# Output product 4 by a second Strassen level, its quarters in a bank of their own, and ReLUs and x's sums at other steps

## The chip, the cores and the metric

The kernel runs on one core of a Trainium2 chip. The time is the device time of one execution in microseconds (us), and the number compared is the median over several executions. Four engines matter here: TensorE (PE, with PEld for its weight loads), VectorE (DVE), ScalarE (ACT) and GpSimd (POOL). SyncE (SP) starts the DMA transfers that read, ScalarE's queue those that write the output.

## The reference, cut to what matters

```python
kv  = einsum('bhsd,bhse->bhde', k, v)          # q, k, v: (8, 8, 576, 64)
out = einsum('bhsd,bhde->bhse', q, kv)         # no softmax
out = out / sqrt(mean(out*out, -1) + 1e-6) * g_norm
x = out.transpose(0, 2, 1, 3).reshape(4608, 512)
h = x @ w_in                                   # 512 -> 2048
g = maximum(0.01 * h, h)
return g @ w_out                               # 2048 -> 512
```

Everything is float32. The two large products, x by w_in and g by w_out, take most of the time.

## The kernel before

The 4608 tokens are worked on in nine blocks of 512. Block 0 goes the plain way (`first_block`). In blocks 1 to 8 (the loop variable i) the 2048 columns of h are taken in four chunks c of 512, so that a chunk has an h product (512 x 512 by 512 x 512) and an output product of the same size, which is added to the block's four output quarters. I number the output products n = 4(i - 1) + c. They wait in `o_queue`: product n begins at the third step (`LAG` = 2 steps) of the chunk after its h, and ends with the second step of the chunk after that.

Both products are done with Strassen's scheme in Winograd's form: seven products of half size (256 x 256 x 256) in the order `ORDER = (1, 2, 6, 5, 7, 3, 4)` instead of eight. One PSUM bank takes 1, 6, 7 and 4 in turn, a second 2, 5 and 3; since each new product is accumulated on the last in the bank, output quarter 11 is 1 + 2, quarter 12 is 1 + 6 + 5 + 3 and so on, and after each step what stands in the bank is copied out or added to its quarter (`strassen`, `done`). The sums that the scheme needs as operands are made ahead: those of g by GpSimd in `sums_of` (tiles `gs`, 128 x 512), those of w_out once, then kept in DRAM and loaded for each chunk by `sums` in `sides_w2` (tiles `t12` and `t34`, 512 KB each, from SP's queue).

In blocks 2 to 8 the h product has a second level (`product_h_two`): each of the seven steps is again seven products of 128 x 128 blocks, four in one bank (j = 1, 6, 7, 4) and three in another (j = 2, 5, 3), with weights from a ring of five places that SP refills (448 KB each). After each step ScalarE copies (k = 1, 6, 5 and 4, line 951) or VectorE adds (k = 2, 7 and 3, helper `add`, line 636) the seven quarters into `qa` and `qc`. When the seven steps are over, seven sums on VectorE make the four quarters of g, `relu` (line 832, ScalarE) is applied to each, and GpSimd makes the four sums of `sums_of`.

The bank of three has a free fourth column. Output product 2 of the products n = 4 to 29 is done in it by a second level (class `Second`): one quarter product of 128 columns is put behind each h step of a later chunk. So in the order of an output product of that kind the place of product 2 is empty: `(1, 5, 6, None, 7, 3, 4)`. Its inner operands are made by GpSimd: `inner_g` (128 x 128 adds at steps 4 and 6) and, in block 2, `inner_w2`.

A chunk has seven steps t, and the block 28 slots, 7c + t. In a step the program gives out, in this order: one h step; at t = 6 the first of the g sums as well; pieces of the attention of a later block at the slots of `FINE_SLOTS` and `LATE_SLOTS`; at slots 20 to 22 x's inner sums for the next block on VectorE (`sides_x`), at 24 and 25 further inner sums on GpSimd; loads; `inner_g`; then one step of the output product. At the chunk's end the rest of the h product follows: the remaining g sums, the four ReLUs and `sums_of`. `pin` keeps an instruction in program order on its engine; what is not pinned the scheduler places when its operands are ready. All matmuls go through the helper of line 118 and most element-wise sums through line 636, so groups are told apart by the names of their tiles.

| name | what it is |
|---|---|
| h_ha, h_hb, h_hc, h_hd | PSUM banks of h steps (even: ha and hc of four, hb and hd of three quarters) |
| o_a, o_c | PSUM banks of the output products |
| pairs | one tile that holds `qc`, `t12`, `t34` and `gi` (inner sums of g) |
| w_all, stage | w1's ring, `qa` and x's sums |
| g, gs | the quarters of g, and GpSimd's sums of them |

The output quarters of a block are accumulated in SBUF (tag "o", six buffers). ScalarE copies the fresh ones at c = 0 and stores each one (256 KB) after the last product of chunk 3 that goes into it.

Of the kernel before, what the change touches and what calls it, by code (L numbers as in the profile page):

```python
# [23 lines left out]
def kernel(  # L24
# [74 lines left out]
    NW = U * NE * P  # L99
    w1_all = consts.tile([P, 2 * NC * NW], F32, name="w1_all")  # L100
    stage = consts.tile([P, 3 * NW], F32, name="stage")
    pairs = consts.tile([P, 4 * NW], F32, name="pairs")
    g_all = [consts.tile([P, 4 * U * N2], F32, name=f"g_{i}") for i in range(2)]

    def view(t, lo, *shape):
# [79 lines left out]
    zeros = view(g_all[0], 0, NT)  # L185
    nc.vector.memset(zeros[:, :64], 0.0)
    nc.vector.memset(zeros[:, 64:], 0.0)
    ident = consts.tile([P, P], F32, name="ident")

    def make_ident():  # L190
        pin(nc.gpsimd.memset(ident, 1.0))
# [448 lines left out]
    def sides_w1(c):  # L640
# [9 lines left out]
        def more():  # L650
# [5 lines left out]

    w2_dram = [[dram.tile([P, 2, U, N2], F32, name=f"w2_{c}_{i}") for i in range(2)]
               for c in range(NC)]
    t12, t34 = pair(2, 2, U, N2), pair(3, 2, U, N2)
    writes = []  # L660

    def sides_w2(n):

        c = n % NC
        b11, b12 = w2_sb[0][c][:, :, :N2], w2_sb[0][c][:, :, N2:]
        b21, b22 = w2_sb[1][c][:, :, :N2], w2_sb[1][c][:, :, N2:]

        def sums(i):  # L670
            t = (t12, t34)[i]
            if n >= NC:
                pin(nc.sync.dma_start(t, w2_dram[c][i]))
                return
            if i == 0:
                add(nc.gpsimd, t[:, 0], b12, b11, True)
                add(nc.gpsimd, t[:, 1], b22, t[:, 0], True)
            else:
                add(nc.gpsimd, t[:, 0], b22, b12, True)
                add(nc.gpsimd, t[:, 1], b21, t12[:, 1], True)  # L680
            if (n, i) == (NC - 1, 1):

                writes.append((w2_dram[c][i], t))
            else:
                pin(nc.sync.dma_start(w2_dram[c][i], t))
        return {1: b11, 2: b21, 3: b22, 5: t12[:, 0], 6: t12[:, 1], 7: t34[:, 0],
                4: t34[:, 1]}, sums
# [49 lines left out]
    def read(to):  # L737
        nonlocal n_read
        while n_read < min(to, len(reads)):
# [5 lines left out]
    qc = pair(0, 4, 3, P)  # L745
    xt1 = [work.tile([P, 2, N2], F32, tag="xt1", name="xt1"),
           view(w1_all, RING * NG + 24 * P, 2, N2)]
    xt24 = [work.tile([P, 2, 2, N2], F32, tag="xt24", name="xt24"),
            view(w1_all, RING * NG + 16 * P, 2, 2, N2)]
    xi = view(stage, 0, 3, 7, P)  # L750

    def sides_x(i):


        x = xTs.pop(i)
        b11, b12 = x[:, :2, :N2], x[:, :2, N2:]
        b21, b22 = x[:, 2:, :N2], x[:, 2:, N2:]
        home = i % 2 if i > 1 else 0
        t1, t2, t4 = xt1[home], xt24[home][:, 0], xt24[home][:, 1]
        if i == 1:  # L760
            t4 = opool.tile([P, 2, N2], F32, tag="o", name="xt4", bufs=6)
        t3 = b12
        sides = {1: b11, 2: b21, 3: b22, 4: t4, 5: t1, 6: t2, 7: t3}

        def sums():
            for t, a, b in ((t1, b12, b11), (t2, b22, t1), (t3, b22, b12), (t4, b21, t2)):
                add(nc.vector, t, a, b, True)
                yield

        batches, quarters, at = [], {k: {} for k in ORDER}, 0  # L770
        upper, lower = (x[:, h:h + 2, :].rearrange("p r (t v n) -> p t r v n", t=2, v=2)
                        for h in (0, 2))
        for js, y in (((1, 7), upper), ((2, 3), lower),
                      ((6, 4), xt24[home].rearrange("p t r (v n) -> p t r v n", v=2)),
                      ((5,), t1.rearrange("p r (v n) -> p r v n", v=2).unsqueeze(1))):
            terms = [y[:, :, r, v, :] for r in range(2) for v in range(2)]
            terms += [xi[:, k, at:at + len(js), :] for k in range(3)]
            batches.append(terms)
            for n, j in enumerate(js):
                for k, term in zip((1, 7, 2, 3, 5, 6, 4), terms):  # L780
                    quarters[k][j] = term[:, n, :]
            at += len(js)

        def inner(kind):
            for y11, y12, y21, y22, t1, t2, t4 in batches:
                if kind == 0:
                    add(nc.gpsimd, t1, y12, y11, True)
                    add(nc.gpsimd, t2, y22, t1, True)
                elif kind == 1:
                    add(nc.gpsimd, y12, y22, y12, True)  # L790
                else:
                    add(nc.gpsimd, t4, y21, t2, True)

        return sides, quarters, sums(), inner

    def strassen(tags, left, right, done, order=ORDER, pieces=None):

# [1 line left out]
        for i in order:  # L801
# [21 lines left out]
            for part in range(2):  # L823
                for r in range(2):
                    matmul(bank[:, part, :], lhsT=left(i, part, r), rhs=right(i, part, r),
                           start=i in FRESH and part == 0 and r == 0, stop=(r == 1),
                           skip_group_check=True)
            done(i, bank.rearrange("p u (v n) -> p (u v) n", v=2))
            yield

    def relu(t, src=None):
        nc.scalar.activation(t, t if src is None else src, func=AF.Prelu, alpha=SLOPE)  # L832

    def g_of(c):

# [42 lines left out]

    gi = view(pairs, 12 * P, 4, P)

    def inner_w2(c):
        y = w2_sb[1][c]
# [7 lines left out]

    def inner_g(c, half):

        g = g_of(c)[3]
        a11, a21, a12, a22 = (g[:, n, :] for n in range(4))
        s1, s2, s3, s4 = (gi[:, n, :] for n in range(4))
        if half == 0:
            add(nc.gpsimd, s1, a21, a22)
            add(nc.gpsimd, s2, s1, a11, True)  # L900
        else:
            add(nc.gpsimd, s3, a11, a21, True)
            add(nc.gpsimd, s4, a12, s2, True)

    class Second:
# [17 lines left out]
        def done(self, k, bank):  # L923
# [3 lines left out]
            if self.n % NC == NC - 1 and k == ORDER[-1]:  # L927
                self.finish("11", self.o)

    def product_h_two(i, c, quarters, to, second):  # L930

        n0 = 7 * ((i - 2) * NC + c)
# [4 lines left out]
        for t, k in enumerate(ORDER):  # L937
            for js, tags, q in zip(GROUPS, (("ha", "hc"), ("hb", "hd")), (qa, qc)):
# [9 lines left out]
                at, fresh = into[k]  # L948
                bank = banks[tag][:, :len(js), :]
                if fresh:  # L950
                    nc.scalar.copy(q[:, at], bank)  # L951
                else:
                    add(nc.vector, q[:, at], bank, q[:, at])
                if len(js) < 4 and second:
# [11 lines left out]
        yield  # L966
        add(nc.vector, g21, g21, qc[:, :, 1, :])
        add(nc.vector, g21, g21, qc[:, :, 2, :])
        for t in (g11, g12, g22, g21):
            relu(t)  # L970
        sums_of(c, to)

    def product_o(n, g_sides, os, finish, second):

        c = n % NC
        w_sides, _ = sides_w2(n)
        sums = sides_w2(n + 1)[1] if n + 1 < NC * (NB - 1) else lambda i: None
        if c == 0:

            for key in ("12", "22", "11", "21"):  # L980
                os[key] = opool.tile([P, 2, N2], F32, tag="o", name=f"o{key}", bufs=6)


        pieces = ((0, slice(0, N2)), (1, slice(0, P)), (1, slice(P, N2))) \
            if n + 1 == NC * (NB - 1) else None
# [2 lines left out]

        def done(i, bank):
            key, fresh = into[i]  # L990
            if isinstance(bank, list):
                for at, (end, (part, cols)) in enumerate(zip(bank, pieces)):
                    to = os[key][:, part, cols]
# [8 lines left out]
                nc.scalar.copy(to, bank)  # L1002
            else:
                add(nc.vector, to, bank, to)
            if c == NC - 1 and i in (2, 7, 3, 4):
                finish(key, os[key])

            if i == (6 if second else 5):
                sums(0)
            elif i == 4:  # L1010
                sums(1)


        yield from strassen((("oa", "oc"), ("oc", "oa"))[n % 2], lambda i, part, r: g_sides[i][:, 2 * r + part, :],
                            lambda i, part, r: w_sides[i][:, r, :], done,
                           (1, 5, 6, None, 7, 3, 4) if second else ORDER,
                           pieces=pieces)

    def go(steps, n=None):
        while n is None or n > 0:  # L1020
# [16 lines left out]
    def first_block(between):  # L1037
# [26 lines left out]
                       start=(now[2] == 0), stop=(n == 2 * NC * U))  # L1064
            between(n, 1)
        for t in range(4):
            o = opool.tile([P, DM], F32, tag="o", name="o", bufs=6)
            if t % 2:
                nc.scalar.copy(o, accs[t])
            else:  # L1070
# [37 lines left out]
    for part in range(2):  # L1108
# [4 lines left out]
    FINE_SLOTS = {1: 1, 2: 1, 4: 1, 9: 1, 10: 2, 11: 1, 12: 1, 15: 1, 16: 2, 17: 2, 18: 1, 19: 1,  # L1113
                  23: 1, 24: 1, 25: 1, 26: 1}
    LATE_SLOTS = (3, 4)

    LAG = 2

# [1 line left out]
    HELD = (22, 24, 26)  # L1120
    o_queue, waited = collections.deque(), 0

    seconds = {}

    def second_of(n):
        if n in seconds:
# [9 lines left out]
    for i in range(1, NB):  # L1136
# [4 lines left out]
        for c in range(NC):  # L1141
# [3 lines left out]
            for t in range(7):  # L1145
                slot = 7 * c + t
                go(h_steps, 1)
                if not one:

                    if t == 6:  # L1150
                        go(h_steps, 1)
                    if slot in LATE_SLOTS:
                        go(late, 1)
                    for _ in range(FINE_SLOTS.get(slot, 0)):
                        go(a_steps, 1)
                    if i + 1 < NB:
                        if slot == 20:
                            x_sides, new_quarters, sums, inner = sides_x(i + 1)
                        if slot in (20, 21, 22):
                            go(sums, 2 if slot == 20 else 1)  # L1160
                        if slot == 24:
                            inner(0)
                        elif slot == 25:
                            inner(1)
                    load_some()

                now = (i - 1) * NC + c
                if now - 1 in seconds:
                    for half in range(2):
                        if t == (6 if half else 4):  # L1170
                            inner_g((now - 1) % NC, half)
                    if t == 5 and now <= 2 * NC:
                        inner_w2((now - 1) % NC)
                if slot == 4 and not one:
                    while writes:
                        pin(nc.sync.dma_start(*writes.pop()))
# [32 lines left out]
            for _ in range(2 if i == NB - 1 and c == NC - 1 else 0):  # L1209
                go(h_steps, 1)  # L1210
                go_o()
            go(h_steps)
            if c == NC - 1 and i + 1 < NB:
                inner(2)
                quarters = new_quarters
            if one:
                read((2, 4, RING, RING)[c])
# [37 lines left out]
```

## Time and profile before

| | |
|---|---|
| median of 4 runs | 916.98 us (916.88 to 917.17) |
| the profiled execution, its own time | 917.17 us |
| span of the profile | 915.5 us |
| PE busy | 908.7 us, 99% |
| DVE busy | 628.3 us, 69% |
| ACT busy | 327.6 us, 36% |
| POOL busy | 366.7 us, 40% |
| DMA | 200 MB, 219 GB/s over the span |

A row of the timeline reads: start in us, length, engine, line, operation, output tile <- inputs, shape, and xN where N neighbouring instructions are put together; a bracket tells of idle time before it and of whom it waited for. A row of a table by windows reads: the stretch, its length, then busy time with the number of instructions for PE, PEld, DVE, ACT and POOL, the granted TensorE clock (1.00 is full), the busy share of the DMA engines and GB/s. A float32 matmul is done in several passes and is recorded as more than one matmul; the text counts recorded ones.

### The profile page before, as it was taken

The page shows a single profiled execution, that of the slowest core. Times are in us where ns is not written, and L with a number is a line of the kernel's source. Part 1 is how long each engine was busy: PE and PEld are TensorE (multiplying, and loading weights), DVE is VectorE, ACT ScalarE, POOL GpSimd, SP SyncE. Part 2 cuts the span into 40 slices and gives each one's busy share as a digit, 9 for nine tenths or more (in the row PEclk, how much of TensorE's full clock was granted, in tenths as well). Part 3 has the DMA queues.
Part 4 walks back from the last instruction along what each step waited for, and adds up shares of the span by engine and source line. Part 5 has one row for each costly group of instructions (what it writes and reads, how often), then busy time and mean ns, then how long its engine had stood idle before and what let it go on. Part 6 is the DMA issues. An engine that isn't in the chain of part 4 may idle for free.

```text
span 915.5 us, 18030 instructions
## 1 busy us (share of the span) xinstructions
PE 908.7 (99%) x6976; PEld 775.6 (85%) x6976; DVE 628.3 (69%) x1168; ACT 327.6 (36%) x645; POOL 366.7 (40%) x440
## 2 busy tenths in 40 slices
PE   8999999999999999999999999999999999999998
PEld 5444448888998999899999999999999999999997
DVE  5876985587457876587756786678659755755565
ACT  5454433242135233533343324332343333223330
POOL 2000246967633472226321642264226422642222
PEclk9999999999999999999999999999999999999999
DMA  9999908885598778876986689657765576567632
GB/s 277 220 234 246 264 23 274 270 280 167 183 372 266 224 212 266 234 230 215 257 257 216 219 250 271 223 177 227 228 184 175 187 222 199 179 193 223 197 107 92
DMA packets 90228, 200.05 MB, mean 219 GB/s; under 512 B 9888, under 2 KB 42272, under 8 KB 90144
## 3 DMA queue, kind: packets, MB, share of 16 engines
q1 hardware_dynamic: 79680, 187.04, 68.5%
q10 hardware_dynamic: 10016, 10.69, 3.4%
q8 instruction: 55, 0.90, 0.4%
q0 software_dynamic: 448, 1.18, 0.3%
q14 instruction: 29, 0.24, 0.1%
HBM read 172.39 MB, written 26.48 MB: 217 GB/s over the span
## 4 chain that ended last, share of the span: by engine, by line
PE 96%; DMA 2%; DVE 1%; issue 0%; ACT 0%; POOL 0%; ACTq 0%; DVEq 0%; POOLq 0%
PE o_a L118 19%; PE o_c L118 18%; PE h_ha L118 11%; PE h_hb L118 11%; PE h_hc L118 8%; PE h_hd L118 8%; PE o_acc L118 6%; PE h_ps L118 6%; PE o_ps L118 3%; PE h_a L118 2%; PE h_b L118 1%; PE h_c L118 1%; PE h_d L118 1%; PE kv_ps L118 1%; DMA pairs<-in_v_dram 1%; DMA v_in<-in_v_dram 1%
## 5 line engine op out<-in xcount | busy, mean ns | idle before, releaser
L636 POOL TENSOR_TENSOR gs<-g 128x512 f32<-128x512 f32 x64 | 81.7, 1277 | 253.2 <-ACT g L832 253.2
L832 ACT ACTIVATE g<-g 128x512 f32<-128x512 f32 x124 | 78.2, 631 | 132.0 <-DVE g L636 132.0
L951 ACT COPY w_all<-h_ha 128x512 f32<-128x512 f32 x84 | 48.9, 582 | 173.9 <-PE h_ha L118 151.8
L118 PE MATMUL o_a<-pairs,gs 128*128 128x256 f32 x384 | 91.3, 381 | 0.0
L118 PE MATMUL o_c<-pairs,gs 128*128 128x256 f32 x376 | 89.2, 380 | 0.0
L636 DVE TENSOR_TENSOR o<-h_hb,o 128x128 f32<-128x128 f32 x104 | 29.8, 287 | 83.3 <-ACT pairs L951 83.2
L118 PEld LDWEIGHTS o_a<-pairs,gs 128*128 128x128 f32 x384 | 69.8, 190 | 9.2 <-POOL pairs L636 1.2
L636 DVE TENSOR_TENSOR o<-o_c,o 128x512 f32<-128x512 f32 (+1 forms) x91 | 61.1, 672 | 23.9 <-PE o_c L118 23.6
L118 PEld LDWEIGHTS o_c<-pairs,gs 128*128 128x128 f32 x376 | 68.3, 190 | 7.7
L636 DVE TENSOR_TENSOR o<-o_a,o 128x512 f32<-128x512 f32 x75 | 51.2, 683 | 28.2 <-PE o_a L118 28.1
L118 PE MATMUL h_ha<-stage,w_all 128*128 128x128 f32 x448 | 59.6, 276 | 0.0
L118 PEld LDWEIGHTS h_ha<-stage,w_all 128*128 128x128 f32 x448 | 56.6, 192 | 3.0 <-issue 0.7
L118 PE MATMUL h_ps<-xT,w_all 128*128 128x512 f32 (+1 forms) x136 | 58.1, 571 | 0.3 <-DVE w_all L258 0.3
L118 PE MATMUL o_acc<-w,g 128*128 128x512 f32 x128 | 57.7, 595 | 0.0
L636 DVE TENSOR_TENSOR g<-g,pairs 128x512 f32<-128x512 f32 x84 | 55.6, 689 | 1.9
L636 POOL TENSOR_TENSOR pairs<-g 128x128 f32<-128x128 f32 x52 | 23.7, 455 | 77.3 <-PE h_hb L118 48.5
L118 PEld LDWEIGHTS h_ps<-xT,w_all 128*128 128x128 f32 x136 | 25.4, 190 | 29.0 <-issue 26.1
L118 PEld LDWEIGHTS o_acc<-w,g 128*128 128x128 f32 x128 | 24.1, 190 | 30.2 <-issue 29.9
L636 DVE TENSOR_TENSOR w_all<-h_hc,w_all 128x512 f32<-128x512 f32 x56 | 38.3, 684 | 15.9 <-PE h_hc L118 15.8
L636 DVE TENSOR_TENSOR o<-h_hd,o 128x128 f32<-128x128 f32 x78 | 22.1, 283 | 38.2 <-ACT pairs L951 38.1
L118 PE MATMUL h_hb<-stage,w_all 128*128 128x128 f32 x336 | 46.7, 275 | 0.0
L951 ACT COPY pairs<-h_hb 128x384 f32<-128x384 f32 x84 | 39.9, 475 | 13.5 <-PE h_hb L118 12.6
(229 smaller groups left out, 2227.6 us busy)
## 6 DMA issues: line engine op xcount, KB each, us to landing
w_all<-w SPq DMA_DIRECT2D x196, 448.0 KB, 4.2
pairs<-w SPq DMA_DIRECT2D x56, 512.0 KB, 4.2
out_dram<-o ACTq DMA_DIRECT2D x35, 256.0 KB, 4.6
v_in<-in_v_dram SPq DMA_DIRECT2D x29, 288.0 KB, 5.2
k_in<-in_k_dram SPq DMA_DIRECT2D x28, 288.0 KB, 4.7
q_in<-in_q_dram SPq DMA_DIRECT2D x56, 144.0 KB, 6.1
q_in<-in_q_dram SPq DMA_DIRECT2D x56, 140.0 KB, 5.9
w<-stage SPq DMA_DIRECT2D x12, 512.0 KB, 4.5
```

The source lines that it names most:

```text
L118: pin(nc.tensor.matmul(*args, **kw))
L636: ins = eng.tensor_tensor(out_, a, b_, op=ALU.subtract if minus else ALU.add)
L832: nc.scalar.activation(t, t if src is None else src, func=AF.Prelu, alpha=SLOPE)
L951: nc.scalar.copy(q[:, at], bank)
```

## The change

1. Output product 4 of the products n = 8 to 28 (those of blocks 3 to 8, but for the last three) is done by a second level as well, in the new class `Fourth`: seven quarter products of 128 columns in one PSUM bank, taken from the tag of the output product's own first bank. They come in four groups: 1, 2 and 5 at t = 1 of the second chunk after the product's h, 6 and 3 there behind product 1 of the next output product, 7 at t = 3, 4 at t = 4 (`FOURTH_AT`). Columns of the bank are used again, so a group needs the one before to be read out. Product 7 no longer shares an accumulation with it; it is kept in a tile of its own, "7", and added to quarters 22 and 21 in chunk 3. The order of the output product becomes `(1, None, 6, 5, 7, 3, None)`.
2. Its inner operands: of w_out, `inner_w4` (GpSimd, once per chunk in block 2), stored in `w4_dram` and loaded again for each chunk in two pieces (256 and 192 KB); of g, `inner_g` now makes both halves at once (128 x 2 x 128), the second half at step 5 instead of 6. The tile `pairs` grows by four blocks of 128 columns.
3. `h_rest`: the ReLUs and `sums_of` are given out at t = 0 of the next chunk, behind the first h step there with its copies, and copies and ReLUs are pinned, so that ScalarE does them in program order. (Block 1 and the last chunk are as before.)
4. x's inner sums go to slots 22, 24 (two) and 25 instead of 20 (two), 21 and 22; GpSimd's inner sums for x are spread over slots 24, 25 and 26 and slot 0 of the next block.
5. The output tiles have four buffers and a tag "o11" with two in place of six; the identity matrix of the transposes shares a tile of x's sums.

```diff
@@ sides_w2
-            if n >= NC:
-                pin(nc.sync.dma_start(t, w2_dram[c][i]))
+            if n >= NC and i:
+                if row != 1:
+                    pin(nc.sync.dma_start(t[:, 0], w2_dram[c][i][:, 0]))
...
+                pin(nc.sync.dma_start(f4, w4_dram[c][:, :4, :]))
+                pin(nc.sync.dma_start(f4_more, w4_dram[c][:, 4:, :]))
+                return
...
@@ strassen
+            if behind and i == 1:
+                behind()
             done(i, bank.rearrange("p u (v n) -> p (u v) n", v=2))
...
@@ inner_w4 and inner_g
+        y11, y12, y21, y22 = (f4[:, k, :] for k in range(4))
+        t1, t3, t2 = (f4_more[:, k, :] for k in range(3))
+        add(nc.gpsimd, t1, y12, y11, True)
...
-        a11, a21, a12, a22 = (g[:, n, :] for n in range(4))
-        s1, s2, s3, s4 = (gi[:, n, :] for n in range(4))
+        a11, a21, a12, a22 = (g[:, n, 2:, :] for n in range(4))
+        s1, s2, s3, s4 = (gi_two[:, :, n * P:n * P + P] for n in range(4))
...
+    class Fourth:
+        STEPS = (1, 2, 5), (6, 3), (7,), (4,)
+        COLUMN = {1: 0, 6: 0, 7: 0, 4: 0, 2: 1, 5: 2, 3: 2}
...
+        def step(self, at):
+            if at == 0:
+                self.bank = ps_m.tile([P, 4, P], F32, tag=self.tag, name=f"f_{self.tag}")
+            for k in self.STEPS[at]:
+                matmul(self.bank[:, self.COLUMN[k], :], lhsT=self.left[k], rhs=self.right[k],
+                       start=(k == 1), stop=True, skip_group_check=True)
+            for k in self.STEPS[at]:
+                bank = self.bank[:, self.COLUMN[k], :]
+                v, s = INTO[k]
+                to = self.o_of("21")[:, v, s * P:s * P + P]
+                if self.n % NC == 0 and k in (1, 5, 6, 4):
+                    nc.scalar.copy(to, bank)
+                else:
+                    add(nc.vector, to, bank, to)
+            if at == 3:
+                self.last()
@@ product_h_two
-                    nc.scalar.copy(q[:, at], bank)
+                    pin(nc.scalar.copy(q[:, at], bank))
...
+        yield
         for t in (g11, g12, g22, g21):
-            relu(t)
+            pin(relu(t))
         sums_of(c, to)
@@ product_o
+            if fourth and i == 7:
+                key, fresh = "7", True
...
+            if fourth and i == 7:
+                if c == NC - 1 or not four(n + 1):
+                    add(nc.vector, os["22"], os["22"], os["7"])
...
+        def last():
+            sums(1, 1)
+            if c == NC - 1 or not four(n + 1):
+                add(nc.vector, os["21"], os["21"], os["7"])
...
+        if fourth or four(n - 1):
+            order = (1, None, 6, 5, 7, 3, None if fourth else 4)
...
@@ the loop
+    FOURTH_AT = {1: 0, 3: 2, 4: 3}
...
+                    if t == 0:
+                        go(h_rest)
+                    if slot == 0 and inner_rest:
+                        inner_rest(2)
+                    if t in FOURTH_AT and four((i - 1) * NC + c - 2):
+                        fourths[(i - 1) * NC + c - 2].step(FOURTH_AT[t])
...
-                        if slot in (20, 21, 22):
-                            go(sums, 2 if slot == 20 else 1)
+                        if slot in (22, 24, 25):
+                            go(sums, 2 if slot == 24 else 1)
                         if slot == 24:
-                            inner(0)
+                            inner(0, (1, 3))
                         elif slot == 25:
+                            inner(0, (0,))
+                        elif slot == 26:
+                            inner(0, (2,))
                             inner(1)
...
-                        if t == (6 if half else 4):
+                        if t == (5 if half else 4):
...
-            go(h_steps)
+            if one or (i, c) == (NB - 1, NC - 1):
+                go(h_steps)
+            else:
+                go(h_steps, 3)
+                h_rest = h_steps
```

## The prediction

> **What bounds the kernel now.** I read the page first, then the stages, then TensorE's own timeline.
>
> ```profile
> span 915.5 us, 18030 instructions
> PE 908.7 (99%) x6976; PEld 775.6 (85%) x6976; DVE 628.3 (69%) x1168; ACT 327.6 (36%) x645; POOL 366.7 (40%) x440
> PEclk9999999999999999999999999999999999999999
> ```
> ```profile
> 430.00:530.00 100.00, 100.00 (x871) 92.82 (x871) 72.55 (x141) 36.58 (x74) 41.05 (x52) 1.00 0.79 237
> ```
> TensorE is busy all the time at full clock, and the stage from 430 to 530 us has no gap in it. A pipelined PE can look busy while it waits, so the starts decide:
>
> ```profile
> 527.16 1.05 PE L118 MATMUL h_ha<-stage,w_all 128*128 128x128 f32 x8
> 528.05 0.83 PE L118 MATMUL h_hb<-stage,w_all 128*128 128x128 f32 x6
> 528.72 0.39 PE L118 MATMUL h_hb<-w,pairs 128*128 128x128 f32 x2
> 528.94 1.89 PE L118 MATMUL o_c<-w,g 128*128 128x256 f32 x8
> 530.67 1.05 PE L118 MATMUL h_hc<-stage,w_all 128*128 128x128 f32 x8
> ```
> An h step (16 recorded matmuls of 128 columns) takes 528.94 - 527.16 = 1.78 us, 0.1113 each; a whole output product (8 of 256) takes 530.67 - 528.94 = 1.73, 0.216 each. A chunk without attention is 7 x 1.78 + 6 x 1.73 = 22.84; the rows have 22.87 (520.13 to 543.00). So TensorE streams, and every other engine matters only through a wait that it does not yet have. The chunk boundary is where it comes nearest to one:
>
> ```profile
> 519.58 0.29 DVE L636 TENSOR_TENSOR o<-h_hb,o 128x128 f32<-128x128 f32 x1 [1.80 <-ACT pairs L951]
> 519.79 0.68 DVE L636 TENSOR_TENSOR g<-w_all 128x512 f32<-128x512 f32 x1
> 520.39 0.69 DVE L636 TENSOR_TENSOR g<-w_all,pairs 128x512 f32<-128x512 f32 x1
> 520.99 0.68 DVE L636 TENSOR_TENSOR o<-o_a,o 128x512 f32<-128x512 f32 x1
> 521.59 1.48 DVE L636 TENSOR_TENSOR g<-g,w_all 128x512 f32<-128x512 f32 x2
> 523.10 2.02 DVE L636 TENSOR_TENSOR g<-g,pairs 128x512 f32<-128x512 f32 x3
> 526.18 0.29 DVE L636 TENSOR_TENSOR o<-h_hb,o 128x128 f32<-128x128 f32 x1 [1.06 <-ACT pairs L951]
> ```
> Here h4 of the old chunk is emptied, seven sums make g, and only then may ScalarE overwrite the first quarters. Call G the end of the seven sums after the chunk's start: 525.12 - 520.13 = 4.99.
>
> Last, VectorE beside GpSimd. The same sum of two SBUF operands takes 0.69 with GpSimd idle and 1.14 beside its add:
>
> ```profile
> 496.21 0.69 DVE L636 TENSOR_TENSOR w_all<-xT,w_all 128x512 f32<-128x512 f32 x1
> ...
> 505.29 1.14 DVE L636 TENSOR_TENSOR w_all<-xT,w_all 128x512 f32<-128x512 f32 x1
> ```
> ```profile
> 504.61 1.28 POOL L636 TENSOR_TENSOR gs<-g 128x512 f32<-128x512 f32 x1
> ```
>
> **The gain on TensorE.** Output product 4 of n = 8 to 28 (21 chunks) goes from 8 x 0.216 = 1.73 to seven quarter products of two recorded matmuls, 14 x 0.1113 = 1.56. 21 x 0.17 = **3.55 us less**. The form is that of the h rows, so the price is measured.
>
> The Trainium skill ("TensorE: Matmul & The Clock Gate", Back-to-back issue gap) speaks against this: in a stream of weight loads and matmuls it gives some 81 ns per pass at N=128, against 56 ns for the bare matmul. Two such passes per recorded matmul, an estimate from that page, would make the product 14 x 0.162 = 2.27 and the change 11 us dearer. The rows, which do change weights each time, have 0.1113, and I go by them.
>
> **The new chunk, step by step** (us from its start, TensorE unhindered): h1 to 1.78, product 3 to 3.51, h2 5.29, quarters 1, 2, 5 of product 4 to 5.96, h6 7.74, product 1 9.47, quarters 6, 3 9.91, h5 11.69, quarter 7 11.91, h7 13.69, quarter 4 13.91, product 6 15.64, h3 17.42, product 5 19.15, h4 20.93, product 7 22.66. Two things are nearer than before: h6 comes 1.06 earlier after h1 (a short step stands where product 4 was), and each group of quarters needs the group before it read out of the bank.
>
> *VectorE, moved and added.* A 128-column add is 0.28, 0.20 apart when independent, about 0.33 when it waits for the one before (0.20 plus the 0.13 by which dependent g sums, 0.73 apart, exceed independent ones). Seven for one add of 0.68: some 1.3 us more per chunk, of 28 us idle in 100. Per block two 128x512 adds (0.73) bring the separate 1+6+7 to outputs 22 and 21.
>
> *ReLUs.* In the order of the built program both copies of h1 now stand before the four ReLUs, but the second waits for the last g sum, so the ReLUs end at G + 2.7 (copy 0.47, ReLUs 0.53 apart) where they ended about G + 0.67. Behind them wait GpSimd's sums: the second is ready at G + 2.7 + 2.6, 10.3 for G = 4.99, and product 6 reads it at 13.91. Hidden until G is 8.6; then the loss begins one for one. The copy itself gains: h1's quarter is added at G + 0.8 (copy 0.46, add 0.28, handing over 0.03 each), where the rows have 526.47 - 520.13 = 6.34.
>
> *x's sums.* They leave steps 20 to 22 for 22, 24 and 25. This relieves chunk 3's start (two sums stood before its g sums), and loads its end.
>
> Two limits follow. h6's second bank (6.85) needs that quarter added: G + 0.80 <= 6.85, **G <= 6.05**. And quarter 7 (11.69) needs quarters 6 and 3 added. In chunk 0 VectorE has in line from G + 0.55: h1's quarter 0.2, product 3 0.6, h2 0.6 + 0.47 + 0.2, three quarters 0.86, a transpose 1.09, h6's quarter 0.2, a transpose 1.09, then 0.33 + 0.28: G + 6.34, **G <= 5.35**.
>
> *G by chunk.* Chunk 1: 543.00 has 547.56, 4.56, plus 0.73 for one of the new adds = 5.3; one transpose less stands before its quarters, ready at 10.9 of 11.69. Chunk 2: about 4.5; quarter 6 is copied by ScalarE behind the square root, ready near 11.55, barely in time. Chunk 3: 4.56; attention's 2 us of matmuls stand between, ready 13.1 of 13.9.
>
> Chunk 0 is late. Chunk 3 before it (block 4, 384 wide, length now 24.87): h5's quarter is added by 14.8. Then VectorE has no gap: quarter 7 0.2, transpose and reduce 1.07, two x sums 0.9 + 0.6, h7 1.27, quarter 4 0.2, transpose and reduce 1.07, x sum 0.9 (GpSimd beside two of the three), product 6 0.6, h3 1.27: 22.9, reciprocal to 23.1. On ScalarE both spreads (0.92), which wait for it, stand before both copies of h4 (0.95): h4's quarter is added from 25.0, which is 0.13 in chunk 0; the rows have -0.55. GpSimd's adds for x, held up by the last x sum, end with the two-part ones (0.73 each) near 1.65, so the first g sums lie beside them: +0.66. G = 4.99 + 0.68 + 0.66 = 6.33, TensorE stands 0.98 in all. For 320 columns (into block 4) transposes, reduces and spreads are some 0.38 less: 0.6. For 448 (into 6) some 0.33 more: 1.3. Into block 7 there are no transposes and the first limit holds: 6.9 - 6.05 = 0.85. Sum **3.7**. No row shows TensorE waking from such a wait; 0.03 (VectorE after ScalarE, 479.47 to 479.50) and 0.20 (ScalarE after TensorE) bound it, I take 0.1 for seven waits: **0.7**.
>
> "SBUF — State Buffer" (Who interferes with whom) says that a two-input SBUF operation of VectorE contends with any GpSimd operation that reads SBUF, and that this is an exclusive lock. Were the loser to stand for a whole GpSimd add of 0.73, two g sums in four chunks would cost 5.8 by that estimate, where I have 2.6; 1.14 against 0.69 is nearer to mine.
>
> *At nothing.* GpSimd's inner g sums go from 0.456 to 0.73 (its 128x256 rows), 1.1 us per chunk; GpSimd is 41 of 100 busy, and the quarters read them a chunk later; gone, they cost one for one. The four inner sums of w2 (block 2, 4 x 0.46) end by 14.6, their store and reload (4.5 each) by 23.3, needed at 28. On SP product 4's weights (256 + 192 KB, 4.2 to land) are asked for at 13.91 and needed 14 us later; the split loads of pairs 5 to 7 have a chunk too. The ring read behind each waiting load goes up to 1.8 late, and the ring is five steps, 16 us, deep. The rotation of the output tiles leaves 13 us for a store of 4.6. The identity's new home touches the start alone.
>
> Sum: -3.55 + 3.7 + 0.7 = **+0.9**. The profiled execution took 917.17 (span 915.5 and 1.7 around it), 0.2 over the median 916.98: 918.1 there, **917.9** as median.
>
> **Rivals.** *VectorE keeps up.* If spreads and x sums fall without the queue I laid out, and GpSimd is done by the boundary, G stays near 5.3 and stalls are under 1.2: 913.4 to 914.7, say 914.2. For it: VectorE idles 1.80 us before 519.58. Against: the two x sums and two quarters put there are longer than that. *The quarter's round trip binds in every chunk* (the slower side). Each group waits for VectorE, which waits for TensorE. Chunk 2 has 0.14 to spare and chunk 1 0.8. If each of 21 products loses 0.25 more, +5.3 on mine: 923; alone, from 0.17 it eats the gain, and with the chunk-0 stalls from 0.05 it is over 0.2%. For it: `DVE o L636 <- ACT pairs L951: 121.2, 91, 3.2` among the waits, VectorE standing behind ScalarE before such adds. Against: the same seconds of product 2 stall nothing today. *ReLUs late*, GpSimd's second sum after product 6: needs G over 8.6, then 1 us each in four chunks, 922. *Nothing happens*: the form is not used; excluded, the built program has the quarters.
>
> **Chances.** My own case 0.50 (915.9 to 919.9), VectorE keeps up 0.20, round trip 0.25, ReLUs 0.05. A measurement tells 0.2%, 1.8 us, from no change: under 915.1 faster, over 918.8 slower. My case splits 0.02, 0.34, 0.14; the first rival is faster but for 0.01, the second slower but for 0.03, the third 0.05 slower: faster 0.21, same 0.38, slower 0.41. The range leaves out a tenth at each side: 914.2 to 921.8.
>
> **What would show it.** Right: after, a product 4 group of seven with 14 matmuls 0.111 apart; stalls of 0.5 to 1.5 in the first chunk of blocks 4 to 7, at h6's second bank and quarter 7, released by VectorE; the ReLUs after both copies. Wrong: stalls spread over all 21 chunks, or at product 6 behind GpSimd, or none at all.

## The result and the profile after

The changed kernel takes 918.68 us (median; 917.96 to 920.42), the kernel before 916.88: a ratio of 1.0024, 95% interval 1.0013 to 1.0034. So it is slower, by 1.8 us by the medians and 2.2 by the ratio, where 0.9 was forecast; that is inside the range and on the side that was forecast. The profile page after:

```profile
span 917.0 us, 18591 instructions
PE 908.0 (99%) x7102; PEld 777.2 (85%) x7102; DVE 662.1 (72%) x1282; ACT 327.4 (36%) x669; POOL 418.7 (46%) x456
PE 89%; DVE 6%; DMA 2%; issue 1%; ACT 1%; POOL 1%; SPq 0%; DVEq 0%; ACTq 0%; POOLq 0%
```

The last line is the chain that ended last, by engine: VectorE has 6% of it where it had 1%. TensorE's busy time fell by only 0.7 us; as the prediction says, its busy share shows no stall, so I take the starts. The same table by windows (stretch, length, busy time of PE, PEld, DVE, ACT, POOL, clock, DMA share, GB/s) now shows a gap in TensorE from 430 to 530 us, where there was none (from 330 to 430 us it has another, a wait for a load that is told below):

```profile
430.00:530.00 100.00, 99.46 (x892) 92.73 (x891) 78.58 (x163) 37.72 (x82) 44.15 (x49) 1.00 0.77 242
```

It lies in the first chunk of block 5, which begins at 520.19. TensorE's timeline there:

```profile
526.15 1.06 PE L118 MATMUL h_ha<-stage,w_all 128*128 128x128 f32 x8
527.75 0.94 PE L118 MATMUL h_hb<-stage,w_all 128*128 128x128 f32 x6 [0.54 <-DVE o L637]
...
532.48 0.39 PE L118 MATMUL h_hd<-w,pairs 128*128 128x128 f32 x2
533.22 0.49 PE L118 MATMUL f_oa<-stage,pairs 128*128 128x128 f32 x2 [0.34 <-DVE o L637]
```

The two stalls are the two limits of the prediction: h6's second bank (8 matmuls should take 0.89, they take 1.60 from start to start: 0.71), then quarter 7 (0.74 for 0.22: 0.52). VectorE's timeline shows what both wait for:

```profile
520.29 0.29 DVE L637 TENSOR_TENSOR o<-h_hb,o 128x128 f32<-128x128 f32 x1 [1.31 <-ACT pairs L1013]
520.50 1.19 DVE L637 TENSOR_TENSOR g<-w_all 128x512 f32<-128x512 f32 x1
521.61 1.21 DVE L637 TENSOR_TENSOR g<-w_all,pairs 128x512 f32<-128x512 f32 x1
...
523.35 1.40 DVE L637 TENSOR_TENSOR g<-g,w_all 128x512 f32<-128x512 f32 x2
524.79 2.02 DVE L637 TENSOR_TENSOR g<-g,pairs 128x512 f32<-128x512 f32 x3
527.40 0.29 DVE L637 TENSOR_TENSOR o<-h_hb,o 128x128 f32<-128x128 f32 x1 [0.60 <-ACT pairs L1013]
```

The sums end at 526.81, so G is 6.62 (4.99 before). Two things made that: h4's quarter is added only at 520.29, and the first two sums take 1.2 us each for 0.68. GpSimd's rows at the same time:

```profile
519.32 1.13 POOL L637 TENSOR_TENSOR w_all<-w_all 128x256 f32<-128x256 f32 x2
520.42 0.72 POOL L637 TENSOR_TENSOR pairs<-g 128x256 f32<-128x256 f32 x1
521.11 1.17 POOL L637 TENSOR_TENSOR pairs<-g,pairs 128x256 f32<-128x256 f32 x1
```

These rows show VectorE and GpSimd taking turns. VectorE's first sum begins while GpSimd's add of 520.42 runs, which ends at 521.14; the sum ends at 521.69, 0.55 us later. The second begins during the next add, which ends at 522.28, and ends at 522.82. That next add had itself begun during the first sum and took 1.17 us for 0.72. The other profiles agree: of 379 sums of 128 x 512 with both operands in SBUF that begin while 0.14 us or more of a GpSimd add is left (twelve profiles, from block 2 on), 376 end 0.55 us after that add does, however much of it was left. In the other three both begin within 0.02 us, the sum takes its 0.68, and it is GpSimd's add that is late. So a sum pays for what is left of the add that it meets, and no fixed factor. The 951 sums of this size that begin beside such an add with one operand in PSUM take 0.62 to 0.69 us.

**Where the 2 us came from.** The starts of the chunks (TensorE's first h matmul of each) repeat within 0.02 us wherever two kernels have the same work. The opening, up to the first h step of block 2, does not: it ended between 226.9 and 228.9 us over the twelve profiles of this study (one execution of each kernel), with no pattern by kernel that I see. I therefore compare the stretch from that step to the last h step. It is 660.00 us before and 662.00 after. By chunks: where nothing waits (all chunks 2, most chunks 1) a chunk with the quarters is 0.164 us shorter (22.70 for 22.87, rounded), 21 times: -3.44. The first chunks of blocks 4 to 7 take 0.23, 1.42, 1.39 and 0.80 more than that, +3.84. Block 3 gives +0.24 in its first chunk and +0.87 in its second. The last chunks of blocks 3 to 6 wait 0.11, 0.14, 0.17 and 0.48; in block 7 a stall of 0.40 that the kernel before has is gone: +0.50 in all. The sum is +2.01.

### The profile page after: what moved, and what is told of

The parts are those of the page before. It is cut to its first block, busy times and chain, and to the rows that moved or that the text cites. A ratio compares the mean times of both kernels' runs of the same rounds, so it can differ in the third digit from the quotient of the medians.

```text
span 917.0 us, 18591 instructions
## 1 busy us (share of the span) xinstructions
PE 908.0 (99%) x7102; PEld 777.2 (85%) x7102; DVE 662.1 (72%) x1282; ACT 327.4 (36%) x669; POOL 418.7 (46%) x456
## 4 chain that ended last, share of the span: by engine, by line
PE 89%; DVE 6%; DMA 2%; issue 1%; ACT 1%; POOL 1%; SPq 0%; DVEq 0%; ACTq 0%; POOLq 0%
PE o_a L118 15%; PE o_c L118 15%; PE h_ha L118 10%; PE h_hb L118 10%; PE h_hc L118 7%; PE h_hd L118 7%; PE o_acc L118 6%; PE h_ps L118 6%; PE o_ps L118 3%; PE f_oa L118 2%; PE f_oc L118 2%; PE h_a L118 2%; PE h_b L118 2%; DVE g L637 1%; DVE o L637 1%; PE h_c L118 1%
## 5 line engine op out<-in xcount | busy, mean ns | idle before, releaser
L853 ACT ACTIVATE g<-g 128x512 f32<-128x512 f32 x124 | 69.2, 623 | 32.7 <-DVE g L637 32.7
L637 DVE TENSOR_TENSOR o<-o_c,o 128x512 f32<-128x512 f32 (+1 forms) x81 | 54.0, 667 | 19.9 <-PE o_c L118 19.7
L637 DVE TENSOR_TENSOR o<-o_a,o 128x512 f32<-128x512 f32 x64 | 43.6, 682 | 22.8 <-PE o_a L118 22.7
L637 POOL TENSOR_TENSOR pairs<-w 128x512 f32<-128x512 f32 x4 | 5.3, 1329 | 98.3 <-DMA stage<-in_moe_w_out_dram 98.3
L637 POOL TENSOR_TENSOR pairs<-g 128x256 f32<-128x256 f32 x52 | 39.7, 764 | 15.0 <-PE h_hb L118 13.4
```

The costliest lines, as they stand in the source:

```text
L637: ins = eng.tensor_tensor(out_, a, b_, op=ALU.subtract if minus else ALU.add)
L853: return nc.scalar.activation(t, t if src is None else src, func=AF.Prelu, alpha=SLOPE)
```

## The experiments

The table has the stretch of every run against the kernel before, split by the chunk of the block (blocks 3 to 8) in which it was won or lost; without any stall the columns of the quarters would be -0.8, -0.8, -1.0 and -0.8.

| run | chunk 0 | chunk 1 | chunk 2 | chunk 3 | sum, us |
|---|---|---|---|---|---|
| the change | 3.24 | 0.05 | -0.98 | -0.32 | 2.00 |
| xsums_back | -0.58 | -0.21 | -0.98 | 1.99 | 0.23 |
| no_quarters | 0.39 | 0.00 | 0.00 | 1.14 | 1.54 |
| relus_early | 9.24 | 1.93 | -0.77 | -0.48 | 9.92 |
| no_inner1 | 0.20 | -0.79 | -0.98 | -0.32 | -1.89 |
| relus_alone | 0.00 | 0.00 | 0.00 | -0.40 | -0.40 |
| x_last_later | 3.31 | -0.82 | -0.98 | -0.30 | 1.22 |
| quarter7_later | 1.88 | -0.10 | -0.98 | 7.14 | 7.94 |
| three_moves | 3.26 | -0.82 | -0.98 | 1.48 | 2.95 |
| two_moves | -0.52 | -0.81 | -0.98 | 2.02 | -0.29 |
| quarters_not_in_3 | -0.52 | -0.82 | -0.98 | -0.40 | -2.72 |

(Block 2 is the same in all, but for 0.22 in no_inner1, which its sum leaves out.)

### x's sums back in their place: xsums_back

```diff
-                        if slot in (22, 24, 25):
-                            go(sums, 2 if slot == 24 else 1)
+                        if slot in (20, 21, 22):
+                            go(sums, 2 if slot == 20 else 1)
```

> The changed kernel with x's inner sums on VectorE back at slots 20 to 22; all else as changed. My theory (VectorE is late into the first chunk of blocks 4 to 7 because two more x sums stand at the end of chunk 3, and the g sums then lie beside GpSimd): TensorE's stalls in those first chunks, 3.84 us in the changed kernel's profile by chunk lengths (0.23 + 1.42 + 1.39 + 0.80), fall below 1.0; the 0.4 us before product 3 in chunk 3 of block 7 returns, and chunk 3 of blocks 3 to 6 may lose up to 0.4 each: 916.0 to 917.5 us. Rival (the seven quarters and GpSimd's wider adds make VectorE late wherever x's sums stand): the stalls stay, 918.2 to 919.5 us.

917.29 us, ratio 1.0002 (0.9987 to 1.0017). The first chunks of blocks 4 to 8 stream: 22.70 each. My theory holds there; the quarters alone do not make those chunks late. But chunk 3 costs more than I had allowed: quarter 7 waits 0.31, 0.35, 0.37 and, in block 6, 1.60 us. TensorE and VectorE there:

```profile
698.90 0.39 PE L118 MATMUL h_hd<-w,pairs 128*128 128x128 f32 x2
700.61 0.49 PE L118 MATMUL f_oc<-stage,pairs 128*128 128x128 f32 x2 [1.32 <-DVE o L637]
```
```profile
696.80 3.24 DVE L373 TENSOR_TENSOR sum<-sum,sq 128x512 f32<-128x512 f32 x2
699.96 0.60 DVE L637 TENSOR_TENSOR o<-f_oc,o 128x128 f32<-128x128 f32 x2
```

The read-out of quarters 6 and 3 stands behind two sums of the attention, 3.24 us (2.10 in the kernel before). Each of the two meets one of GpSimd's sums of g, which come later now because the ReLUs do:

```profile
696.10 1.71 POOL L637 TENSOR_TENSOR gs<-gs,g 128x512 f32<-128x512 f32 x1
697.77 1.72 POOL L637 TENSOR_TENSOR gs<-g 128x512 f32<-128x512 f32 x1
```

The second of these ends at 699.49, and VectorE's two sums at 700.04, again 0.55 later. In block 7 chunk 3 waits 0.57 for VectorE, at product 1 and the quarters behind it. So moving x's sums took a wait of 2.3 us out of chunks 3 and put 3.8 into chunks 0.

### The moves without the quarters: no_quarters and relus_alone

```diff
     def four(n):
-        return 2 * NC <= n < NC * (NB - 1) - 3
+        return False
...
-            elif i == 4 and NC <= n < 2 * NC:
+            elif False:
```

relus_alone has the edit of xsums_back besides.

> The changed kernel without the second level for product 4 (it runs whole, as before); ReLUs, x's sums and the two-part sums of g as changed. My theory: product 4 whole puts h6 1.06 us later after h1, so the limit of the first chunks goes from G 6.05 to 7.1 us, above the 6.6 reached, and no quarter waits: no stalls in first chunks, and the 0.39 us in chunk 3 of block 7 is gone: 916.3 to 917.0 us, chunks of 22.87. Rival (the moved sums and ReLUs cost by themselves): stalls of about 1 us stay in the first chunks of blocks 5 to 7, 918.5 to 920 us.

> The changed kernel without the second level for product 4 and with x's inner sums back at slots 20 to 22: what is left of the change are the ReLUs behind the next first copies, the wider adds of GpSimd and the output tiles. My theory: these cost nothing and give nothing, the 0.39 us in chunk 3 of block 7 is as in the kernel before: chunks of 22.87, 916.5 to 917.6 us beside 917.1 of the kernel before. Rival (the ReLUs' new place, or GpSimd's wider adds, cost by themselves): over 918 us, with stalls in first chunks.

no_quarters takes 918.92 us, ratio 1.0018 (1.0001 to 1.0035): the rival was nearer in size, but not in place. The first chunks have 0.10 at most, as my theory says, and 1.5 us are lost at the end of chunk 3, in blocks 4 to 6. TensorE and ScalarE at that of block 6:

```profile
711.19 1.89 PE L118 MATMUL o_a<-pairs,gs 128*128 128x256 f32 x8
713.79 0.49 PE L118 MATMUL h_ha<-xT,w_all 128*128 128x128 f32 x2 [0.70 <-ACT w_all L1013]
```
```profile
712.12 1.14 ACT L395 COPY spread<-rms 128x512 f32<-128x512 f32 x2 [2.40 <-DVE rms L391]
713.16 0.58 ACT L1013 COPY w_all<-h_ha 128x512 f32<-128x512 f32 x1
```

The next h1 needs the bank of h4, whose copy stands on ScalarE behind the spreads, and these wait for VectorE's reciprocal, which x's two sums hold up. This is the chain that the prediction laid out for chunk 3's end; I had carried it only to h4's quarter, not to the next h1. relus_alone (916.76 us, ratio 0.9996, 0.9984 to 1.0009) has no such wait: with the sums in their old place the ReLUs' move and the wider adds cost nothing, and chunk 3 of block 7 has lost its 0.40, which I had not expected. VectorE and TensorE there in the kernel before:

```profile
787.26 1.29 DVE L636 TENSOR_TENSOR xT<-xT 128x512 f32<-128x512 f32 x1
788.47 0.68 DVE L636 TENSOR_TENSOR o<-o_a,o 128x512 f32<-128x512 f32 x1
```
```profile
789.20 1.99 PE L118 MATMUL o_a<-w,g 128*128 128x256 f32 x8
```

One of x's sums meets GpSimd's first sum of g, which runs from 786.73 to 788.00, and takes 1.29 us; the bank of product 1 is read out behind it, and TensorE stands until then. In relus_alone GpSimd's sums begin about 2 us later, behind the ReLUs, and the same sum takes 0.68.

### The ReLUs ahead of the copies: relus_early

```diff
-            if one or (i, c) == (NB - 1, NC - 1):
+            if True:
                 go(h_steps)
```

> The changed kernel with the four ReLUs (and GpSimd's sums behind them) given out at the chunk's end again, ahead of the next chunk's first copies on ScalarE. My theory: both copies of h1 then wait for the last ReLU, h1's quarter is added at about G + 1.75 instead of G + 0.8, so h6's second bank stalls more, by up to 1 us in each first chunk and some tenths in second chunks: 920 to 924 us. Rival (what costs is that ReLUs and so GpSimd's sums come later): stalls shrink, 916.5 to 918 us.

928.05 us, ratio 1.0108 (1.0088 to 1.0128): the direction is my theory's, the size beyond it. TensorE and ScalarE in the first chunk of block 5:

```profile
527.50 0.39 PE L118 MATMUL f_oa<-stage,pairs 128*128 128x128 f32 x2
529.69 1.16 PE L118 MATMUL h_ha<-stage,w_all 128*128 128x128 f32 x8 [1.81 <-ACT w_all L1013]
```
```profile
526.54 1.30 ACT L853 ACTIVATE g<-g 128x512 f32<-128x512 f32 x2 [1.35 <-DVE g L637]
528.54 0.63 ACT L853 ACTIVATE g<-g 128x512 f32<-128x512 f32 x1 [0.70 <-DVE g L637]
529.07 0.57 ACT L1013 COPY w_all<-h_ha 128x512 f32<-128x512 f32 x1
```

I had reckoned with h6's second bank; already its first has to wait, since the copy of h1's first bank stands behind the last ReLU too. (The kernel before, whose copies were not pinned, had that copy between its ReLUs.) With quarters and pins, the ReLUs' move is worth 8 us.

### GpSimd out of the way: no_inner1

```diff
                             inner(0, (2,))
-                            inner(1)
```

> The changed kernel without the third of GpSimd's four inner sums for x in blocks 2 to 7 (four adds per block, 2.5 us of GpSimd, left out; part of x's inner sums is missing from the output). GpSimd is then done before the first two g sums of a first chunk. My theory: these two sums fall from 1.2 to 0.68 us, G from 6.6 to about 5.6, and the stall of the first chunk of blocks 5 and 6 from 1.4 to 0.3 us: 915.3 to 916.6 us. Rival (VectorE's own queue alone makes G, contention nothing): 918.2 to 919 us.

915.33 us, ratio 0.9981 (0.9965 to 0.9997). GpSimd is done 1.1 us before the first sum, and VectorE's rows are:

```profile
519.45 0.68 DVE L637 TENSOR_TENSOR g<-w_all 128x512 f32<-128x512 f32 x1
520.05 0.68 DVE L637 TENSOR_TENSOR g<-w_all,pairs 128x512 f32<-128x512 f32 x1
...
522.69 2.02 DVE L637 TENSOR_TENSOR g<-g,pairs 128x512 f32<-128x512 f32 x3
```

G is 5.58 (the chunk begins at 519.13), between the two limits of 5.35 and 6.05: h6 no longer waits, quarter 7 waits 0.37. The first chunks lose 3.0 us less. So with x's sums where the change has them, the contention of these adds is most of what the first chunks pay.

### GpSimd's order in block 3: x_last_later

```diff
-                    if slot == 0 and inner_rest:
+                    if slot == 2 and inner_rest:
```

> The changed kernel with GpSimd's last inner sums for x given out at slot 2 instead of slot 0 of the next block, behind the inner sums of w_out for product 4 (first chunk of block 3). My theory: chunk 1 of block 3 waits 0.87 us for weights whose store and load start late because GpSimd comes late to those sums; they come 2.9 us earlier now, and the chunk goes from 24.96 to about 24.0: 917.2 to 918.2 us. Rival (the load is late by SyncE's queue or by the store itself): the chunk keeps over 0.6 us of it, 918.4 to 919 us.

The stall in question is that of the second chunk of block 3 in the changed kernel, on TensorE, with GpSimd's and SyncE's rows before it (sums for x, then the first inner sums of w_out; the store, and the reload behind it):

```profile
353.99 0.39 PE L118 MATMUL h_hd<-w,g 128*128 128x128 f32 x2
355.01 1.96 PE L118 MATMUL o_c<-pairs,g 128*128 128x256 f32 x8 [0.64 <-DMA pairs<-w]
```
```profile
340.70 1.87 POOL L637 TENSOR_TENSOR stage<-xT,stage 128x256 f32<-128x256 f32 x2
342.54 1.14 POOL L637 TENSOR_TENSOR stage<-w_all,stage 128x256 f32<-128x256 f32 x2
343.63 1.34 POOL L637 TENSOR_TENSOR stage<-pairs 128x128 f32<-128x128 f32 x2
```
```profile
345.95 0.34 SPq L1091 DMA_DIRECT2D w<-pairs  x1
...
349.20 0.42 SPq L686 DMA_DIRECT2D pairs<-w  x1
```

In the run the sums come first, and the whole product 4 follows without a gap:

```profile
355.47 0.39 PE L118 MATMUL h_hd<-w,g 128*128 128x128 f32 x2
355.69 1.89 PE L118 MATMUL o_c<-pairs,g 128*128 128x256 f32 x8
```

The chunk went from 24.96 to 24.09, as my theory says. The time of the whole, 918.79 us (ratio 1.0017, 1.0007 to 1.0027), does not show it: it is above my band, in the rival's. The opening of its profile is 1.4 us longer than that of the changed kernel; whether its other executions share that is not known.

### The quarters later: quarter7_later and three_moves

```diff
-    FOURTH_AT = {1: 0, 3: 2, 4: 3}
+    FOURTH_AT = {1: 0, 4: 2}
...
-            if behind and i == 1:
-                behind()
+            if behind and i in (1, 6):
+                behind(1 if i == 1 else 3)
```

three_moves has the edits of xsums_back and x_last_later besides.

> The changed kernel with quarter 7 of product 4 one step later (behind h7) and quarter 4 behind product 6; x's sums as changed. My theory: of the stalls of the first chunks the part at quarter 7 goes (0.12 in block 4, 0.6 each in blocks 5 and 6), the part at h6's second bank stays (0.70, 0.68 and 0.59 in blocks 5 to 7), and the small ones in chunks 3 go: 916.6 to 917.7 us. Rival (the wait only moves on, to quarter 4 or to product 5, whose bank has to be read out first): 918.2 to 919.2 us.

> All three together: x's inner sums back at slots 20 to 22, GpSimd's last sums for x at slot 2, quarter 7 one step later and quarter 4 behind product 6. My theory: no first chunk stalls on VectorE but block 3's 0.24 us, the quarter stalls of chunks 3 (0.31 to 1.60 us with the sums back) go with the later quarters, and 0.57 us in chunk 3 of block 7 stay: the gain of 21 x 0.17 less about 0.6: 913.2 to 914.8 us. Rival (VectorE is too full in chunk 3, the quarters stall at their later place too): 915.5 to 917 us.

924.51 us, ratio 1.0079 (1.0066 to 1.0092), and 920.07 us, ratio 1.0036 (1.0024 to 1.0048): the rivals have the mechanism, and both times lie above even their bands. The wait only moved to quarter 4. In chunk 3 of block 4 of quarter7_later:

```profile
511.93 1.89 PE L118 MATMUL o_a<-pairs,gs 128*128 128x256 f32 x8
514.98 0.49 PE L118 MATMUL f_oc<-pairs,g 128*128 128x128 f32 x2 [1.15 <-DVE o L637]
```
```profile
513.38 0.68 DVE L637 TENSOR_TENSOR w_all<-h_ha,w_all 128x512 f32<-128x512 f32 x1
513.98 0.54 DVE L637 TENSOR_TENSOR pairs<-h_hb,pairs 128x384 f32<-128x384 f32 x1
514.45 0.28 DVE L637 TENSOR_TENSOR o<-h_hb,o 128x128 f32<-128x128 f32 x1
514.65 0.28 DVE L637 TENSOR_TENSOR o<-f_oc,o 128x128 f32<-128x128 f32 x1
```

Behind h7, quarter 7's read-out stands behind h7's three adds on VectorE (1.27 us), and these behind two of x's sums that end at 513.4; TensorE gave it only product 6 (1.73) for all that. In three_moves, where x's sums stand elsewhere, the first chunks of blocks 4 to 7 wait at quarter 4 instead (0.86 to 1.08 us above the streaming chunk each), behind sums of the attention and h7's adds. I had counted the slack that quarter 7 gains and not the place that its read-out loses.

### Quarters where VectorE has room: two_moves and quarters_not_in_3

two_moves joins the edits of xsums_back and x_last_later; quarters_not_in_3 adds to them:

```diff
     def four(n):
-        return 2 * NC <= n < NC * (NB - 1) - 3
+        return 2 * NC <= n < NC * (NB - 1) - 3 and n % NC != 1
...
-            if c == 0 and fresh:
+            if fresh and (c == 0 or key == "7" and not four(n - 1)):
                 nc.scalar.copy(to, bank)
```

> The changed kernel with x's inner sums back at slots 20 to 22 and GpSimd's last sums for x at slot 2; the quarters where the change put them. My theory: the costs add up by place: no first chunk stalls but block 3's 0.24 us, chunk 1 of block 3 goes from 24.69 to 24.09, the quarter-7 waits in chunks 3 stay (0.31, 0.35, 0.37, 1.60 and 0.57 us above the streaming chunk): 0.4 us below the kernel before, 916.3 to 917.2 us. Rival (another place takes the wait over): 917.5 us or more.

> As the run beside it (x's sums at slots 20 to 22, GpSimd's last sums at slot 2), but the products 4 whose quarters fall in a chunk 3 (n = 9, 13, 17, 21, 25) run whole as before, and the separate product 7 starts anew behind them (two more 128x512 adds and one copy per block). My theory: quarters cost nothing in chunks 0 to 2 and only wait in chunk 3, where VectorE is full; 16 x 0.17 = 2.7 us of gain, less 0.24 in block 3: 2.5 us below the kernel before, 914.2 to 915.6 us. Rival (the two more adds per block come in chunks 1 and 2, whose quarters had little to spare, and these stall in their place): 915.8 to 917.2 us.

two_moves: 917.74 us, ratio 1.0007 (0.9995 to 1.0020), not told from the kernel before, above my band and in the rival's. No other place takes the wait over, though: its stretch, 0.29 below before, has every chunk within 0.06 of where I expected it (0.30 for 0.24 in block 3's first chunk and 24.09 in its second; 0.32, 0.36, 0.38 and 1.61 at quarter 7 in chunks 3, and 0.58 in block 7). The opening of its profile is 1.0 us longer than that of the kernel before. quarters_not_in_3: 915.25 us, ratio 0.9980 (0.9967 to 0.9993). It is the fastest whole kernel here; no chunk of blocks 4 to 8 waits, and the page has the same TensorE share in a shorter span:

```profile
span 913.3 us, 18515 instructions
PE 906.5 (99%) x7072; PEld 777.0 (85%) x7072; DVE 663.2 (73%) x1257; ACT 329.8 (36%) x674; POOL 414.9 (45%) x456
```

So the quarters are worth their 0.16 us wherever VectorE can read them out in time, and the loss is one of place. What is left of the stalls is 0.29 in block 3's first chunk.

## Why the prediction was right, step by step

**The gain.** 21 x 0.17 = 3.55 was 21 x 0.164 = 3.44. Weights change at each quarter, and the chunk still got shorter by that, so the measurement decides. The estimate that the prediction made from the Trainium skill's "TensorE: Matmul & The Clock Gate" (Back-to-back issue gap), a product of 2.27 us, would have made every chunk 0.54 longer.

**G and the two limits.** Right in mechanism and nearly in size: G 6.62 for 6.33 in block 5; h4's quarter is added from 0.10 us into the chunk where 0.13 was forecast. The difference is contention, 1.04 for the two sums where I took 0.66. The second limit owes its size to luck: its terms add up to G + 6.47 and not to the G + 6.34 that stands there. The rows have G + 6.35 (quarters 6 and 3 are added by 533.16), because the three quarters took 0.72 where I took 0.86. The stalls of blocks 4 to 7 were forecast as 0.6, 1.0, 1.3 and 0.85, with 0.7 of wake-ups over all; they are 0.23, 1.42, 1.39 and 0.80, wake-ups and all. A wake-up is 0.06 from VectorE's end (527.69) to TensorE's start, and the six matmuls behind it take 0.77 from start to start instead of 0.67: 0.16 where I took 0.1, six or so times. The sentence that no row shows TensorE waking is wrong: in chunk 3 of block 7 of the kernel before VectorE ends at 789.15, TensorE starts at 789.20, and its product takes 1.83 instead of 1.73. xsums_back and no_inner1 both show the cause: take away either x's sums or the GpSimd adds beside the g sums, and these stalls go or shrink to a quarter. On contention the prediction weighed the exclusive lock of "SBUF — State Buffer" (Who interferes with whom) and put it aside for a factor, 1.14 against 0.69. The rows agree with the page: the two engines take turns. Even the prediction's own pair does, GpSimd's add ending at 505.89 and the sum at 506.43. What was wrong was the estimate made from the page, that each g sum stands for a whole GpSimd add of 0.73: it stands for what is left of the add, and the two sums took 0.51 and 0.53 more.

**What failed.** First, "The four inner sums of w2 (block 2, 4 x 0.46) end by 14.6, their store and reload (4.5 each) by 23.3, needed at 28", costed at nothing. The last of them fall in the first chunk of block 3, and end 20.1 after its start at 325.81 (the fourth at 345.92). G is 7.1 there and not 4.99, so GpSimd's four sums of g, behind the ReLUs, come about 2 us later; and its last sums for x (2.9 us) stand ahead. (The sum was off by a little, too: 14.6 and twice 4.5 are 23.6.) The reload is asked for at 349.20 and TensorE waits at 354.2: 0.87 us. x_last_later shows it. Second, chunk 3: "attention's 2 us of matmuls stand between, ready 13.1 of 13.9". In block 4 quarters 6 and 3 are read out by 13.9, behind two sums of the attention (2.61 us), and quarter 7 loses 0.14 with its wake-up; it loses 0.11 to 0.17 in each of blocks 3 to 6. Left out altogether was the chain from the reciprocal through the spreads and h4's copy to the next h1, 0.32 in block 6. Together they make 0.90 us. Third, block 3's first chunk, which I took as undisturbed, waits 0.24; it has G 7.1 from VectorE's slow sums there, and in no_inner1 (G 6.1) it has 0.05. Against these stands the 0.40 that chunk 3 of block 7 no longer waits: the sentence that TensorE streams before was drawn from another stage. The unforeseen 1.6 us and 0.1 of gain that did not come, less 0.6 by which the first chunks' stalls were smaller, make the 1.1 between forecast and stretch. So the mechanism was right where most of the loss arose, and that the sum came as near as it did is partly luck: 2.0 us of waits that it had at nothing stand against errors the other way.

**The rivals.** "VectorE keeps up" is out by the stalls. "The round trip binds in every chunk" is out: all chunks 2 and, but for block 3, all chunks 1 stream at full gain, though I saw 0.14 us of room in chunk 2. "ReLUs late" is out: no product waits for GpSimd's sums of g.

## What to carry to other kernels

A cheaper form of a product that needs more read-outs is paid by the engine that reads them out, and the price depends on the place: the same seven quarters, with x's sums in their old place, cost nothing in three chunks of a block and up to 1.6 us in the fourth. Reckon each read-out by where it stands in that engine's program order, not by its own length, and leave the dear places in the old form. When a load or a sum is costed at nothing, follow every queue in front of it, that of the helper engine too.

## What the runs showed of the hardware that I had not expected

Contention between VectorE and GpSimd on SBUF operands decides here, and it is exact: a sum of 128 x 512 with both operands in SBUF takes 0.68 alone, and if it begins while 0.14 us or more of a GpSimd add is left, it ends 0.55 us after that add (1.29 in all in the longest row shown here). So the price of such a meeting can be read off the place in the add at which it falls. And the steady part of the program repeats to 0.02 us per chunk while the opening differs by up to 2 us between the twelve profiles, so that a question of tenths is settled by the chunks of two profiles rather than by the medians.
